# Batch 1 in loaded token order, tails of two batches transposed together, and a new order of the work around them

## The chip, the core and the metric

The kernel runs on one core of a Trainium2 chip. TensorE (PE) multiplies matrices into PSUM, which has eight banks of 128 x 512 float32 per core here; VectorE (DVE), ScalarE (ACT) and GpSimd (POOL) work on tiles in SBUF, the first two also on PSUM. SyncE (SP) and other engines' queues issue transfers (DMA). Each engine runs its own instructions in the order in which they were written, and waits for others by semaphores. The metric is the device time of one execution in microseconds, the median of several; the profile shows one execution, instruction by instruction.

## The reference, cut to what matters

Block-causal attention over 8 batches of 8 heads with 576 tokens of 64 elements, then a gated feed-forward layer over all 4608 tokens.

```python
B, H, S, D = 8, 8, 576, 64
scores = matmul(q, k.T) / sqrt(D)             # per batch and head
scores = where(i // 64 >= j // 64, scores, -1e9)
attn   = exp(scores - max) / (sum + 1e-9)
x      = matmul(attn, v)                      # then (B, S, H*D) -> 4608 x 512
gate   = maximum(x @ w_gate, 0)               # 512 x 1536
val    = x @ w_val                            # 512 x 1536
out    = (gate * val) @ w_out                 # 1536 x 512, float32
```

The order of the tokens matters only where blocks are compared (queries against keys) and in the output rows.

## The kernel before

**Units of work.** A batch has 576 tokens: four full chunks of 128 (the "mains") and 64 more (the "tails"). A head pair is two heads side by side on 128 partitions; there are 32, numbered r = 4 * batch + pair. For each, `scores_all` (before line 480; `scores_of` for batch 0) makes transposed scores with 64-row matmuls (line 464) into three pairs of PSUM banks, ScalarE turns them into exponentials (line 470) in `attnT`, corners above the diagonal are set to zero (`corners`, lines 531 and 532), `head_av` multiplies them with V (line 596; a column of ones gives the sums), and `heads_to_xnat` normalises into `xnat` (lines 544, 545). `to_xT_pe` (line 641) transposes `xnat` on TensorE into `xT`, the feed-forward input with d_model on partitions; from r = 13 on a DMA does it. The tails of batches 0 and 1 have functions of their own: `pe_tails` (line 381) transposes their Q and K, `scores_last` and `scores_tails` make scores, `tails_av` (line 563) and `tails_to_xT` (line 579) the rest. Tails of all batches are gathered in `xTt` and go through the feed-forward layer as a ninth block of 512 tokens.

**The feed-forward layer** is a generator, `ffn_gen` (line 671). For each block of 512 tokens it makes twelve tiles f: four products with `w_gate` and four with `w_val` (line 687) into a pair of banks, relu on ScalarE (line 696), the product of both on VectorE (line 701). Then four output tiles of twelve products each with `w_out` (line 716), copied by VectorE (line 728) and stored. It yields after every four products, so that attention of later batches can be put between: `ffn(n)` runs on to the end of a tile, `ffn_parts(n)` runs n pieces of four. Everything is written out by hand between lines 777 and 977: within an engine, this order is the order of execution.

**Banks.** Banks 0 to 5 are dealt out by `take`, least recently taken first; banks 6 and 7 (`AV`) hold attention outputs and some transposes.

**Loads.** Inputs are float32. They land in a ring of ten `stage` tiles, and POOL casts most of them to bf16 (lines 259, 452, 289, 180). Q, K and V of batches 0 to 3 are loaded with four consecutive tokens per partition (1 KB pieces). A transpose then gives the tokens in the order (j, n), and the copy out of PSUM puts them back in order by reading n and j crosswise (`pe_mains`, line 361). V of batch 1, loaded in the same way, is sorted by products with a selection matrix `sel` (`sort_v`, line 308). The weights come in the order `w_0` (columns 0 to 511 in two halves), `w_1` (columns 512 to 1023, by rows), `w_2`, `w_out`.

**The stretch that the change touches.** After batch 0's attention (up to about 20 us) TensorE runs batch 0's feed-forward work, and between its pieces batch 1's attention (r = 4 to 7), both batches' tails, and the loads and casts of batch 2; from line 926 on a loop over r = 8 to 31 follows, which alternates attention and feed-forward pieces in a fixed pattern.

Of the kernel before, what the change touches and what calls it, by code (L numbers as in the profile page):

```python
# [17 lines left out]
def kernel(  # L18
# [30 lines left out]
    AV = 6  # L49
    taken = [0] * 6  # L50

    def take(n):

        lo = min(range(0, 6, n), key=lambda i: (max(taken[i : i + n]), i))
        taken[lo : lo + n] = [max(taken) + 1] * n
        return banks[:, lo : lo + n, :]

# [42 lines left out]
    sel = consts.tile([128, 2, 516], BF, name="sel")  # L100
# [4 lines left out]
    def constants_tail(i, eng):  # L105

        eng.memset(k_bt[i], 0.0)
        eng.memset(attnT[i][:, :, TAIL + 256 : AW], 0.0)
        eng.memset(attnD[i][:, 256:320], 0.0)
        eng.memset(v_bf[i][:, 4, :, :], 0.0)  # L110
        for hh in range(2):
            eng.memset(v_bf[i][64 * hh : 64 * hh + 64, 4, hh::2, 64:65], 1.0)

    def selection(zero, copy):

        zero(sel, 0.0)
        for c in range(4):
            ps = slice(32 * c, 32 * c + 32)
            copy(
                sel[ps, c % 2].rearrange("p (j m) -> p j m", j=4)[:, :, 0:128:4],  # L120
                ident[ps, None, 32 * c : 32 * c + 32].to_broadcast([32, 4, 32]),
            )

# [34 lines left out]
    class Tails:  # L158


        def load(self):
            self.q, both = new_stage(1024)[0:64], new_stage(1024)
            self.kv = both[:, 0:512], both[:, 512:1024]
            nc.sync.dma_start(
                self.q.rearrange("p (h d) -> p h d", h=16),
                q[0:2, :, 512:576, :].rearrange("b h p d -> p (b h) d"),
            )
            for st, src in zip(self.kv, (k, v)):
                for hh in range(2):
                    nc.sync.dma_start(  # L170
                        st[64 * hh : 64 * hh + 64].rearrange("p (h d) -> p h d", h=8),
                        src[0:2, hh::2, 512:576, :].rearrange("b h p d -> p (b h) d"),
                    )

        def cast(self, b, eng):
            es[b].tl = new_qt()
            eng(es[b].tl, self.q[:, 512 * b : 512 * b + 512])
            for st, diag in zip(self.kv, (k_diag, v_diag)):
                for hh in range(2):
                    eng(  # L180
                        diag(b, hh),
                        st[64 * hh : 64 * hh + 64, 256 * b : 256 * b + 256].rearrange(
                            "p (h d) -> p h d", h=4
                        ),
                    )

    class Early:

        def __init__(self, b):
            self.b = b
            self.m = new_bf()
            self.st = {}
            self.perm = {}
# [67 lines left out]

        def cast_tails(self, engs):
# [21 lines left out]
        def cast_v_packed(self, h0, eng):  # L288
            eng(
                v_p[:, :, 64 * h0 : 64 * h0 + 256].rearrange(  # L290
# [9 lines left out]
        def sort_v(self, h0, engs, out=None):  # L300
# [3 lines left out]
            for odd in range(2):  # L304
                for j in range(4):
                    for g in range(2):
# [4 lines left out]
                            v_p[ps, j, 64 * h0 : 64 * h0 + 256],  # L311
# [39 lines left out]
        def pe_mains(self, hp, evac, out=None):  # L351
            out = out or pair()
            for t in range(2):
# [3 lines left out]
                for j in range(4):  # L357
# [3 lines left out]
                evac[t](  # L361
                    (qTm, kTm)[t][self.b % 2][:, :, hp, :].rearrange(
                        "p c (n j) -> p c n j", j=4
                    ),
                    tp.rearrange("p (j c n) -> p c n j", j=4, c=4),
                )

        def pe_tails(self, evac):

            out = pair()  # L370
            for t in range(2):
                n = (64, 128)[t]
                tp = as_bf(out[:, t, :])[:, 0 : 4 * n].rearrange(
                    "p (h n) -> p h n", h=4
                )
                for hp in range(4):
                    if t == 0:
                        src = self.tl[:, 128 * hp : 128 * hp + 128]
                    else:
                        src = k_bt[self.b % 2][:, hp, :]  # L380
                    nc.tensor.transpose(tp[:, hp, :], src, ident[:n, :n])
                evac[t]((qTt, kTt)[t][self.b % 2], tp)
# [48 lines left out]
    def load_w_half(i, g):  # L431

        sts = []
        for dst, src in ((wg, moe_w_gate), (wv, moe_w_val)):
# [7 lines left out]

    def load_w_in(i):
        cols = slice(512 * i, 512 * i + 512)
        return load_w(wg[i], moe_w_gate[:, cols], 0) + load_w(wv[i], moe_w_val[:, cols], 0)
# [34 lines left out]
    def scores_all(r, tails=True):  # L480
# [3 lines left out]
        sc = [  # L484
            scores(b, hp, pair(), [(0, 0, True)]),
            scores(b, hp, pair(), [(0, 1, True), (384, 3, True)]),
            scores(
                b, hp, pair(),
                [(0, 2, True)]
                + [(256 + 64 * c, c, False) for c in range(4 if tails else 0)],  # L490
            ),
        ]
        for hh in range(2):
            exp(at[:, hh, 0:512], sc[0][:, hh, :])
        exp(at[:, :, 512:1024], sc[1])
        w = 512 if tails else 256
        exp(at[:, :, 1024 : 1024 + w], sc[2][:, :, 0:w])
# [14 lines left out]
    def scores_tails(b):  # L512

        for i in range(2):
# [57 lines left out]
    def tails_of(x):  # L572
# [3 lines left out]
    def tails_to_xT(b, x, evac):  # L576
        tp = as_bf(take(1)[:, 0, :])[:, 0:256].rearrange("p (h n) -> p h n", h=4)
        for hp in range(4):
            nc.tensor.transpose(tp[:, hp, :], x[:, hp, :], ident[:64, :64])
        evac(xTt[:, :, b, :], tp)  # L580
# [35 lines left out]
    def heads_to_xnat(r):  # L616

        blocks = NCH if r >= 8 else 4
        av = banks[:, AV : AV + 2, 0 : 65 * blocks].rearrange(
# [16 lines left out]
    def to_xT_pe(r, evac, bank=None):  # L636
# [3 lines left out]
        for c in range(4):  # L640
            nc.tensor.transpose(br[:, 128 * c : 128 * c + 128], xnat[:, c, :], ident)  # L641
        if b > 1:
            nc.tensor.transpose(br[:, 512:576], xnat[0:64, 4, :], ident[0:64, 0:64])
# [14 lines left out]
    store = []  # L658

    def put(j, s, ob, n0, n1):  # L660
        if j < B:
            r0 = S * j + 128 * s
            (nc.gpsimd if j == 0 else nc.scalar).dma_start(out[r0 : r0 + 128, :], ob)
        else:
            for i in range(2):
# [3 lines left out]
                )  # L669

    def ffn_gen():

        for j in range(B + 1):
# [4 lines left out]
            for fs in groups:  # L678
                out = {f: pair() for f in fs}
                gate = {}  # L680
                steps = [(f, t, c) for f in fs for t in range(2) for c in range(4)]
                if len(fs) > 1:

                    steps.sort(key=lambda step: (step[2] == 3, step[1], step[2]))
# [14 lines left out]
                for f in fs:  # L699
                    h = sb.tile([128, 512], BF, name="hT", bufs=15)  # L700
# [3 lines left out]
                    hT.append(h)  # L704
                yield True
            todo = [[o] for o in outs(j)]
            if j == 0:

                todo = [outs(0)[0:2]] + todo[2:]
            for group in todo:  # L710
                ops = take(len(group))
# [14 lines left out]
                for g, (s, n0, n1) in enumerate(group):  # L726
                    ob = sb.tile([128, 512], FP, name="ob", bufs=3)[:, 0 : n1 - n0]
# [3 lines left out]
                    store.append(lambda j=j, s=s, ob=ob, n=(n0, n1): put(j, s, ob, *n))  # L731
                yield True
# [22 lines left out]
    def ffn_parts(n):  # L755

        for _ in range(n):
            assert next(gen) is False
# [16 lines left out]
    with tc.manual_schedule(engines={E.PE, E.DVE, E.Activation, E.Pool, E.SP}):  # L775
# [7 lines left out]
        w_0 = [load_w_half(0, g) for g in range(2)]  # L783
        w_1 = load_w_in(1)
# [4 lines left out]
        e0.cast_qk(0, 2, (dve, act))  # L789
        e0.pe_mains(0, (dve, act), banks[:, 4:6])  # L790
        junk(2, banks[:, 7])
        constants(1, nc.gpsimd)
        constants_tail(1, nc.gpsimd)
        for h0 in (2, 4, 6):
# [211 lines left out]
```

## Time and profile before

| | us |
|---|---|
| median of 3 runs (369.71 to 371.03) | 369.93 |
| the profiled execution | 370.19 |
| its span, first to last instruction | 368.4 |
| TensorE busy in it | 355.9 |
| VectorE, ScalarE, POOL busy | 165.6, 170.6, 116.2 |

The granted TensorE clock is 1.00 throughout.

How to read the lines that follow. A row of the order of time begins with its start and its length in us, then engine and source line, operation, output and inputs, shape, and how many instructions it joins; in brackets stands how long the engine was idle before, and what ended that. PE is the matmuls, PEld the weight loads that run beside them. A row of a group ends with total busy time and mean ns of one. A row by stretch has the stretch, its length, the busy time of PE, PEld, DVE, ACT and POOL (with counts), the granted clock, the busy share of the DMA engines, and GB/s.

### The profile page before, as it was taken

The page shows a single profiled execution, that of the slowest core. Times are in us where ns is not written, and L with a number is a line of the kernel's source. Part 1 is how long each engine was busy: PE and PEld are TensorE (multiplying, and loading weights), DVE is VectorE, ACT ScalarE, POOL GpSimd, SP SyncE. Part 2 cuts the span into 40 slices and gives each one's busy share as a digit, 9 for nine tenths or more (in the row PEclk, how much of TensorE's full clock was granted, in tenths as well). Part 3 has the DMA queues.
Part 4 walks back from the last instruction along what each step waited for, and adds up shares of the span by engine and source line. Part 5 has one row for each costly group of instructions (what it writes and reads, how often), then busy time and mean ns, then how long its engine had stood idle before and what let it go on. Part 6 is the DMA issues. An engine that isn't in the chain of part 4 may idle for free.

```text
span 368.4 us, 7471 instructions
## 1 busy us (share of the span) xinstructions
PE 355.9 (97%) x2954; PEld 187.1 (51%) x2993; DVE 165.6 (45%) x329; ACT 170.6 (46%) x268; POOL 116.2 (32%) x161
## 2 busy tenths in 40 slices
PE   6889999999999999999999999999999999999995
PEld 2634455556555555555555555555555544444443
DVE  5744444376475543444334443444344433423422
ACT  5833738656665653455445543644364403302310
POOL 5767768175898205810391022000000000000000
PEclk9999999999999999999999999999999999999999
DMA  8999999979999979997599829073201130020013
GB/s 255 289 371 354 376 203 332 165 198 231 195 186 140 140 136 77 179 97 147 87 179 91 137 78 136 19 143 70 88 16 18 46 101 1 3 85 28 2 38 104
DMA packets 139891, 51.02 MB, mean 138 GB/s; under 512 B 119504, under 2 KB 133072, under 8 KB 139856
## 3 DMA queue, kind: packets, MB, share of 16 engines
q1 hardware_dynamic: 78448, 34.29, 40.7%
q0 software_dynamic: 56704, 8.13, 39.9%
q10 hardware_dynamic: 4704, 8.13, 6.3%
q8 instruction: 23, 0.38, 0.5%
q14 instruction: 12, 0.10, 0.1%
HBM read 37.75 MB, written 9.44 MB: 128 GB/s over the span
## 4 chain that ended last, share of the span: by engine, by line
PE 89%; DMA 5%; SPq 2%; ACT 1%; issue 1%; POOL 1%; DVE 0%; ACTq 0%; DVEq 0%; POOLq 0%
PE banks L687 48%; PE banks L716 25%; PE banks L596 7%; PE banks L464 6%; DMA stage<-in_moe_w_val_dram 3%; SPq L223 1%; DMA stage<-in_v_dram 1%; DMA stage<-in_k_dram 1%; PE banks L563 1%; PE banks L308 1%; PE banks L358 1%; ACT attnT L470 0%; PE banks L641 0%; DVE ob L728 0%; POOL wv L452 0%
## 5 line engine op out<-in xcount | busy, mean ns | idle before, releaser
L470 ACT ACTIVATE attnT<-banks 128x1024 bf16<-128x1024 f32 (+1 forms) x118 | 84.9, 804 | 61.8 <-PE banks L464 56.2
L696 ACT ACTIVATE gate_sb<-banks 128x512 bf16<-128x512 f32 x108 | 64.9, 603 | 104.9 <-PE banks L687 104.2
L701 DVE TENSOR_TENSOR hT<-gate_sb,banks 128x512 bf16<-128x512 bf16 x108 | 74.1, 688 | 81.9 <-PE banks L687 77.6
L687 PE MATMUL banks<-xT,wv 128*128 128x512 bf16 x379 | 98.6, 379 | 1.6 <-POOL wv L452 1.2
L687 PE MATMUL banks<-xT,wg 128*128 128x512 bf16 x363 | 97.4, 379 | 1.8 <-ACT v_p L470 0.4
L716 PE MATMUL banks<-wo,hT 128*128 128x512 bf16 (+1 forms) x433 | 96.3, 373 | 0.6
L687 PEld LDWEIGHTS <-wv 128*128 128x128 bf16 x432 | 42.0, 98 | 52.8 <-POOL wv L452 2.8
L716 PEld LDWEIGHTS <-hT 128*128 128x128 bf16 x444 | 42.3, 98 | 46.1
L687 PEld LDWEIGHTS <-wg 128*128 128x128 bf16 x432 | 40.4, 98 | 45.8 <-issue 1.0
L728 DVE COPY ob<-banks 128x512 f32<-128x512 f32 (+1 forms) x37 | 25.1, 677 | 56.2 <-PE banks L716 56.1
L406 POOL DMA_DIRECT2D v_bf<-in_v_dram x16 | 14.3, 904 | 67.5 <-PE banks L596 67.5
L596 PEld LDWEIGHTS <-attnT 128*128 128x128 bf16 x792 | 29.2, 98 | 9.1 <-issue 1.3
L596 PE MATMUL banks<-v_bf,attnT 128*128 128x65 bf16 x792 | 33.6, 194 | 0.2 <-DVE qTm L361 0.2
L464 PE MATMUL banks<-qTm,kTm 64*128 64x512 bf16 (+3 forms) x256 | 25.3, 299 | 2.1 <-ACT attnT L470 1.2
L545 DVE TENSOR_TENSOR xnat<-banks,recip 128x640 bf16<-128x640 f32 (+2 forms) x36 | 25.9, 721 | 1.2
L464 PEld LDWEIGHTS <-kTm 64*128 64x128 bf16 x512 | 16.9, 94 | 11.2 <-issue 1.7
L544 DVE RECIPROCAL recip<-banks 128x10 f32<-128x10 f32 (+3 forms) x38 | 8.0, 210 | 31.4 <-PE banks L596 29.7
L531 DVE MEMSET attnT<- 64x192 uint32 x28 | 6.1, 218 | 19.5 <-ACT attnT L470 18.9
L406 POOL DMA_DIRECT2D k_bf<-in_k_dram x16 | 14.2, 929 | 1.2 <-DMA v_bf<-in_v_dram 1.2
L406 POOL DMA_DIRECT2D q_bf<-in_q_dram x16 | 14.4, 927 | 0.4 <-DMA v_bf<-in_v_dram 0.4
L687 PE MATMUL banks<-xTt,wg 128*128 128x512 bf16 x48 | 12.3, 379 | 0.1
L687 PE MATMUL banks<-xTt,wv 128*128 128x512 bf16 x46 | 12.0, 379 | 0.1
(98 smaller groups left out, 203.2 us busy)
## 6 DMA issues: line engine op xcount, KB each, us to landing
out_dram<-ob ACTq DMA_DIRECT2D x28, 256.0 KB, 2.2
stage<-in_moe_w_gate_dram SPq DMA_DIRECT2D x6, 512.0 KB, 9.4
stage<-in_moe_w_val_dram SPq DMA_DIRECT2D x6, 512.0 KB, 9.7
stage<-in_q_dram SPq DMA_DIRECT2D x6, 512.0 KB, 7.1
stage<-in_k_dram SPq DMA_DIRECT2D x6, 512.0 KB, 8.5
stage<-in_moe_w_out_dram SPq DMA_DIRECT2D x6, 512.0 KB, 9.1
stage<-in_v_dram SPq DMA_DIRECT2D x8, 256.0 KB, 6.0
q_bf<-in_q_dram POOLq DMA_DIRECT2D x16, 128.0 KB, 6.6
```

The source lines that it names most:

```text
L406: nc.gpsimd.dma_start(dst, src[b, :, 128 * c : 128 * c + n, :].rearrange("h p d -> p h d"),)
L464: nc.tensor.matmul(o, kTm[b % 2][ps, c, hp, :], x, start=True, stop=True)
L470: nc.scalar.activation(out, sc, AF.Exp, scale=scale)
L531: eng.memset(three[:, :, :, 0:64], 0.0)
L544: nc.vector.reciprocal(recip, av[:, :, :, 64])
L545: nc.vector.tensor_tensor(out=out, in0=av[:, :, :, 0:64], in1=recip.to_broadcast([rows, heads, n, 64]), op=AX.mult,)
L596: nc.tensor.matmul(av[:, 0, p, :], w, vb[:, c, h, :], start=(p == 0), stop=(c == p), skip_group_check=True,)
L687: nc.tensor.matmul(out[f][:, t, :], (wg, wv)[t][i][:, c, fo : fo + 128], x[:, c, :], start=(c == 0), stop=(c == 3),)
L696: nc.scalar.activation(gate[f], out[f][:, 0, :], AF.Relu)
L701: nc.vector.tensor_tensor(out=h, in0=gate[f], in1=out[f][:, 1, :], op=AX.mult)
L716: nc.tensor.matmul(ops[:, g, 0 : n1 - n0], hT[f][:, 128 * s : 128 * (s + 1)], wo[i][:, f % 4, n0:n1], start=(f == 0), stop=(f == 11),)
L728: nc.vector.tensor_copy(ob, ops[:, g, 0 : n1 - n0])
```

## The change

Line numbers below are those of the profile of before, unless said.

1. **Loaded order for batch 1.** Q and K of batch 1 are copied out of PSUM in an order in which each half chunk of 64 tokens keeps the order (j, n) of its load (`AS_LOADED`); `sel` sorts V into the same order. Blocks of 64 tokens are what the mask compares, so nothing else changes until `to_xT_pe`, which for batch 1 multiplies with a permuted identity `order` and so puts tokens back. POOL builds `order` with one copy at the start.
2. **Tails of batches 0 and 1.** Their Q and K are loaded with four tokens per partition in 1 KB pieces, cast into one `perm` tile, and transposed by eight 128 x 128 transposes (`Tails.pe`) in place of sixteen; six copies on VectorE take them out of PSUM. `kTt` is therefore zeroed at the start (one more memset on DVE, one on POOL). The normalised tails of both batches share one tile `xt` and four transposes.
3. **Whole transposes.** For batches 2 and 3 the fifth transpose of `to_xT_pe` takes all 128 rows.
4. **Weights.** `w_1` is loaded and cast in column halves, as `w_0` and `w_2` are.
5. **Start.** The first K cast is split between ScalarE and POOL, and the copy of the first K in two; one weight cast moves ahead of a V cast on POOL.
6. **The order between batch 0's attention and the loop** is rewritten: batch 1's attention moves earlier and between other feed-forward pieces, `ffn(n)` is replaced by `parts(n)`, eight more products are done ahead of the loop, several copies move from ScalarE to VectorE. `take` skips banks that the feed-forward generator holds. For batch 1 the first two tiles run the products with input rows 0 to 255 first.
7. **Stores and buffers.** The stores of block 0 go from POOL's queue to ScalarE's; `ob` has 4 buffers (3), `hT` 13 (15).

The diff, cut to its core:

```diff
+    AS_LOADED = {(1, hp) for hp in range(4)}
+    def token_order(copy):
+        copy(order.rearrange("p (h n j) -> p h j n", h=2, j=4),
+             ident.rearrange("p (h j n) -> p h j n", h=2, j=4))
...
+        def pe(self, evac):
+            out = pair()
+            for t in range(2):
+                tp = as_bf(out[:, t, :])[:, 0:512]
+                for j in range(4):
+                    nc.tensor.transpose(
+                        tp[:, 128 * j : 128 * j + 128], self.bf[:, t, j, :], ident)
+                tp = tp.rearrange("p (j n b h) -> p j n b h", j=4, b=2, h=4)
+                for b in range(2):
+                    for hh in range(2) if t else (0,):
+                        ps = slice(64 * hh, 64 * hh + 64) if t else slice(0, 128)
+                        dst = kTt[b][ps, :, ps] if t else qTt[b]
+                        evac[t](dst.rearrange("p h (n j) -> p h n j", j=4),
+                                tp[ps, :, :, b, :].rearrange("p j n h -> p h n j"))
...
+                    if (self.b, hp) in AS_LOADED:
+                        dst = dst.rearrange("p c (h j n) -> p c h j n", h=2, j=4)
+                        src = tp.rearrange("p (j c h n) -> p c h j n", j=4, c=4, h=2)
...
-            nc.tensor.transpose(br[:, 512:576], xnat[0:64, 4, :], ident[0:64, 0:64])
+            nc.tensor.transpose(br[:, 512:640], xnat[:, 4, :], ident)
...
-        w_1 = load_w_in(1)
+        w_1 = [load_w_half(1, g) for g in range(2)]
...
-        e0.cast_qk(0, 2, (dve, act))
-        e0.pe_mains(0, (dve, act), banks[:, 4:6])
+        e0.cast_first((dve, act, pool))
+        e0.pe_mains(0, (dve, act), banks[:, 4:6], first=True)
...
+        parts(3)
+        cast_w(w_out[0], pool)
+        e1.pe_mains(0, (dve, dve), banks[:, AV : AV + 2])
+        cast_w(w_out[1], pool)
+        parts(1)
+        e1.load_qk(4, 4)
+        e1.pe_mains(1, (act, dve), banks[:, AV : AV + 2])
+        cast_w(w_out[2], pool)
+        scores_all(4, False)
+        parts(3)
+        corners(4, nc.vector)
+        parts(1)
+        e1.cast_qk(4, 4, (pool, pool))
+        e1.sort_v(0, (act, dve), banks[:, AV : AV + 2])
+        scores_all(5, False)
+        heads_av(4)
+        parts(1)
+        e1.load_v_packed(4)
+        corners(5, nc.vector)
+        parts(1)
+        heads_av(5)
+        parts(1)
+        tails.load()
+        tails.cast_qk(pool)
+        to_xT_pe(4, (act,), None)
+        parts(3)
+        e1.cast_v_packed(4, pool)
+        parts(2)
...
+        e1.pe_mains(2, (dve, dve), banks[:, AV : AV + 2])
+        parts(1)
+        e1.pe_mains(3, (dve, dve), banks[:, AV : AV + 2])
+        scores_all(6, False)
+        tails.pe((dve, dve))
+        corners(6, nc.vector)
+        to_xT_pe(5, (act,), banks[:, AV + 1])
+        scores_all(7, False)
+        e1.sort_v(4, (dve, dve), banks[:, AV : AV + 2])
+        parts(1)
+        corners(7, nc.gpsimd)
+        tails.cast_v(1, pool)
+        parts(2)
+        heads_av(6)
+        scores_last(0)
+        scores_tails(0, (0,))
+        scores_tails(0, (1,))
...
+        to_xT_pe(6, (act,), None)
+        e2.cast_tails((pool, pool))
+        heads_av(7)
+        parts(1)
```

More of the change, by code (lines that the diff above doesn't have):

```diff
@@ L50, with hold @@
     taken = [0] * 6
+    held = set()
     def take(n):
-        lo = min(range(0, 6, n), key=lambda i: (max(taken[i : i + n]), i))
+        free = [i for i in range(0, 6, n) if not held & set(range(i, i + n))]
+        lo = min(free, key=lambda i: (max(taken[i : i + n]), i))
         taken[lo : lo + n] = [max(taken) + 1] * n
+        last[:] = range(lo, lo + n)
         return banks[:, lo : lo + n, :]
+    last = []
+    def hold(bank):
+        held.update(last)
+        return bank
     def pair():
@@ L194, in __init__ @@
             self.b = b
+            self.v_p = (wo[2], v_p)[b % 2]
             self.m = new_bf()
@@ L349, in unpermute, with pe_mains @@
                 )
-        def pe_mains(self, hp, evac, out=None):
+        def pe_mains(self, hp, evac, out=None, which=(0, 1), first=False):
             out = out or pair()
-            for t in range(2):
+            for t in which:
                 tp = as_bf(out[:, t, :])[:, 0:512]
```

310 lines of the change are left out of this document (157 added, 153 removed).

## The prediction, made before the changed kernel ran

> **What bounds the kernel now.** I read the page's busy times and its chain of waits first, then busy times by stretch, then TensorE's order of time from 20 to 90 us, because that is where the diff sits.
>
> ```profile
> PE 355.9 (97%) x2954; PEld 187.1 (51%) x2993; DVE 165.6 (45%) x329; ACT 170.6 (46%) x268; POOL 116.2 (32%) x161
> ...
> PE 89%; DMA 5%; SPq 2%; ACT 1%; issue 1%; POOL 1%; DVE 0%; ACTq 0%; DVEq 0%; POOLq 0%
> ...
> 28.00:86.00 58.00, 56.40 (x574) 31.40 (x583) 28.08 (x57) 32.02 (x54) 36.11 (x45) 1.00 1.01 271
> 86.00:151.00 65.00, 64.57 (x626) 35.59 (x629) 33.76 (x66) 35.90 (x59) 37.62 (x49) 1.00 1.66 154
> ```
>
> TensorE is the bound: 97% busy and 89% of the chain, at a granted clock of 1.00 in both stretches. So an edit can gain in two ways only: fewer or cheaper TensorE instructions, or less waiting of TensorE. After 86 us almost nothing waits (64.57 busy of 65.00), so nothing done there by other engines is worth time. Between 28 and 86 us the busy share hides some waiting, because a matmul's busy time runs past the start of the next one; I therefore read gaps from start to start.
>
> **Part 1: the weights of columns 512 to 1023 (`w_1`) come in column halves.** Before, four transfers bring row halves, so the first feed-forward tile of these columns (f=4) needs all four.
>
> ```profile
> 25.21 1.03 PE L687 MATMUL banks<-xT,wg 128*128 128x512 bf16 x4
> 26.68 0.60 PE L687 MATMUL banks<-xT,wv 128*128 128x512 bf16 x2 [0.44 <-POOL wv L452]
> 28.04 0.60 PE L687 MATMUL banks<-xT,wv 128*128 128x512 bf16 x2 [0.76 <-POOL wv L452]
> 28.48 1.03 PE L687 MATMUL banks<-xT,wg 128*128 128x512 bf16 x4
> 29.34 1.03 PE L687 MATMUL banks<-xT,wv 128*128 128x512 bf16 x4
> ...
> 22.61 0.54 PEld L687 LDWEIGHTS <-wv 128*128 128x128 bf16 x4 [0.61 <-POOL wv L452]
> 22.86 1.04 POOL L452 CAST wg<-stage 128x1024 bf16<-128x1024 f32 x1 [0.31 <-DMA stage<-in_moe_w_gate_dram]
> 26.94 1.04 POOL L452 CAST wv<-stage 128x1024 bf16<-128x1024 f32 x1 [0.32 <-DMA stage<-in_moe_w_val_dram]
> 32.96 1.04 POOL L259 CAST k_bf<-stage 128x1024 bf16<-128x1024 f32 x1 [0.46 <-DMA stage<-in_k_dram]
> ...
> 20.00:24.00 4.00, 3.83 (x18) 1.62 (x18) 1.96 (x4) 1.68 (x3) 3.13 (x3) 1.00 1.05 385
> 28.00:32.00 4.00, 3.96 (x19) 1.84 (x20) 1.38 (x2) 1.20 (x2) 2.63 (x3) 1.00 1.10 348
> ```
>
> Four products take 0.864 us (28.48 to 29.34), so eight take 1.73. The eight of f=4 run from 25.21 to 28.48, 3.27 us: 1.54 us are waits for casts, and the casts wait for loads. After, f=4 and f=5 need only the first two transfers. They land about where the first two land now (the first cast starts at 22.86); the second is cast by about 25.6, and its first use is at 25.21 + 0.86 = 26.07. The gain is the whole 1.54 us.
>
> Its cost: rows of a half are 1 KB long where they were 2 KB. The stretch with 2 KB pieces moves 385 GB/s and the one with 1 KB pieces 348, which is 1.36 against 1.51 us per 512 KB. Four transfers make every later load some 0.6 us late. The nearest user is the first K transpose of batch 1: 44 products after 25.21, plus four transposes, at 34.94. Its cast ends at 34.00 now and would end at 34.6, so 0.3 us of cover are left.
>
> **The opening** I cost at nothing. VectorE gets a memset and a wider one ahead of the first Q cast (0.3 us later), the first K cast and its copy are split (about 0.3 us sooner). Whatever comes of it ends at f=2, whose weight loads wait until 22.61 for a cast that only the loads set. TensorE's idle before that row is the cover; an opening later by more would cost its excess one for one.
>
> **Part 2: fewer and whole transposes on TensorE.** Tails of batches 0 and 1: sixteen transposes, half of them 64 rows high, become eight whole ones. The two last groups of four become one. In batch 2 the fifth transpose of a head pair becomes 128 rows high.
>
> ```profile
> 35.39 0.39 PE L358 MATMUL banks<-ident,q_bf 128*128 128x128 bf16 x4
> 35.61 0.39 PE L358 MATMUL banks<-ident,k_bf 128*128 128x128 bf16 x4
> ...
> 61.59 0.29 PE L381 MATMUL banks<-ident,q_bt 64*128 64x64 bf16 x4
> 61.81 0.40 PE L381 MATMUL banks<-ident,k_bt 128*128 128x128 bf16 x4
> ...
> 62.80 0.38 PE L641 MATMUL banks<-ident,xnat 128*128 128x128 bf16 x4
> ...
> 88.49 0.39 PE L641 MATMUL banks<-ident,xnat 128*128 128x128 bf16 x4
> ...
> 88.94 1.04 PE L687 MATMUL banks<-xT,wg 128*128 128x512 bf16 x4
> ```
>
> Four whole transposes issue in 0.22 us (35.39 to 35.61). The sixteen take 61.59 to 62.80, 1.21 us; eight whole ones take 0.45: gain 0.76. Four narrow ones take the same 0.22 (61.59 to 61.81), so one group less is 0.22. A group of four whole and one narrow takes 0.45 (88.49 to 88.94); five whole take 0.28: 0.17 each, four times 0.68. Together 1.66 us. TensorE is the bound, so all of it counts. The permuted identity replaces the plain one in the same count of instructions: nothing.
>
> **Part 3: the order of batch 1.** The work is the same; what counts is where TensorE waits. Waits that go away, from starts:
>
> ```profile
> 44.26 0.88 PE L464 MATMUL banks<-qTm,kTm 64*128 64x512 bf16 x8
> 45.07 0.48 PE L596 MATMUL banks<-v_bf,attnT 128*128 128x65 bf16 x10
> ...
> 59.84 1.11 PE L464 MATMUL banks<-qTm,kTm 64*128 64x512 bf16 x8
> 60.88 0.78 PE L596 MATMUL banks<-v_bf,attnT 128*128 128x65 bf16 x20
> ...
> 63.51 0.65 PE L464 MATMUL banks<-qTt,kTm 64*128 64x64 bf16 x32
> 64.09 0.78 PE L596 MATMUL banks<-v_bf,attnT 128*128 128x65 bf16 x20
> 64.71 0.38 PE L687 MATMUL banks<-xT,wg 128*128 128x512 bf16 x1
> 65.46 1.24 PE L687 MATMUL banks<-xT,wg 128*128 128x512 bf16 x4 [0.37 <-ACT v_p L470]
> ...
> 70.72 0.86 PE L464 MATMUL banks<-qTt,kTm 64*128 64x64 bf16 x32
> 71.73 0.81 PE L687 MATMUL banks<-xT,wg 128*128 128x512 bf16 x3 [0.16 <-issue]
> ```
>
> Eight score products take 0.81 us unhindered (44.26 to 45.07) and 1.04 at 59.84: 0.23 lost. One product from 64.71 to 65.46 takes 0.75 where 0.216 is due: 0.54. Thirty-two small ones take 0.58 at 63.51 and 1.01 at 70.72: 0.43. Sum 1.20 us, all where tails and two head pairs are crowded behind ScalarE.
>
> Waits that come, because score blocks now follow each other with less between them. The prices hang on these rows:
>
> ```profile
> 60.26 2.49 ACT L470 ACTIVATE attnT<-banks 128x512 bf16<-128x512 f32 x4 [1.32 <-PE banks L464]
> ...
> 62.62 0.48 DVE L382 COPY qTt<-banks 128x256 bf16<-128x256 bf16 x2
> ...
> L361 DVE COPY qTm<-banks 128x512 bf16<-128x512 bf16 x7 | 4.8, 689 | 3.6 <-PE banks L358 3.5
> ...
> L644 DVE COPY xT<-banks 128x512 bf16<-128x512 bf16 x3 | 1.3, 425 | 3.1 <-PE banks L641 3.0
> ```
>
> The exponentials of a head pair start 0.42 us after its scores (59.84, 60.26) and last 2.49. Bounded from both sides, by laying these durations behind the changed order: f=10 takes the banks of the first scores of head pair 4 (0.2 to 0.5); the heads of pair 4 follow the V sort at once (0 to 0.3); those of pair 5 need its last exponential and the zeroing of its corners (0.1 to 0.45); the new tail transposes take the banks of the first scores of pair 6 (0.3 to 0.7); the scores of pair 7 take those of its other scores and of the tails' six copies (0.5 to 1.25); transposing pair 6 right behind its heads needs the normalised tile (0.2 to 0.6); the first product of batch 2 now follows the last transpose of its input directly (0.1 to 0.35). Ends: 1.4 and 4.15 us. The like waits above measure 0.23, 0.54 and 0.43, about 0.4 each; these stand at five places (score blocks of pairs 4 and 5, tails, pair 7, batch 2), so I take 2.0.
>
> One assumption in it: Q and K copies of batch 1 are now read in runs of 16 elements, and I let them take the 425 ns of the contiguous xT copy, not the 689 ns of the old one.
>
> A rule that speaks against this part: the Trainium skill, page TensorEngine Tiling (Array Packing), section PSUM Bottleneck, says to empty PSUM with both ScalarE and VectorE. The change gives both copies of three of batch 1's four head pairs and all six tail copies to VectorE. By my rows that costs no more than the 2.0; by the rule it goes to the upper end, 4.15, which is the second rival below.
>
> POOL loses four stores (ScalarE issues them; between the head pairs it has nothing to do), and the tails' Q and K come in 1 KB pieces instead of 256 B; both only move loads that have slack now.
>
> **Sum.** 1.54 + 1.66 + 1.20 - 2.0 = 2.4 us gained. The profiled execution took 370.19 us with a span of 368.4; it would take 367.8. The median of the runs is 369.93, so I predict 367.5.
>
> **Rivals.** First, *the waits are covered* (chance 0.22): ScalarE and VectorE are about half busy, and between the blocks stand feed-forward products. Only 0.6 us of new waits remain: gain 3.8, 366.1 us. Against it: the score blocks of pairs 6 and 7 have no feed-forward product between them. Second, *the change doesn't quicken the copies, and VectorE and PSUM banks bind* (0.14): copies stay at 689 ns, every new wait goes to its upper end. Gain 4.40 - 4.15 = 0.25: 369.7. Third, *slower: the tails' load takes over* (0.22).
>
> ```profile
> 49.06 1.04 POOL L259 CAST k_bf<-stage 128x1024 bf16<-128x1024 f32 x1 [0.94 <-DMA stage<-in_k_dram]
> ...
> 53.39 0.87 POOL L180 CAST k_bt<-stage 64x256 bf16<-64x256 f32 x2
> ...
> 56.28 0.41 POOL L180 CAST v_bf<-stage 64x256 bf16<-64x256 f32 x1 [1.56 <-DMA stage<-in_v_dram]
> ```
>
> Batch 1 now runs earlier, close behind its loads. POOL casts the tails' Q and K ahead of the second V half, and TensorE transposes them at about 54.4 (from 25.21, 27.6 us of issue and 1.6 of waits lie ahead of them). Casting two tiles of 512 takes some 1.25 us, so it decides from a landing later than 53.2. The last tail piece lands at 56.2 now; had the new ones landed there, 0.6 late, they would be ready at 58.1: 3.7 us lost, net 1.3 slower, 371.2; each further 0.6 us adds as much. For it: K of the second half is cast only at 49.06, 0.94 us after POOL was free. Against it: the larger pieces, and the tails' K was being cast at 53.39 already.
>
> **Chances.** My forecast has 0.42, with its own range 366.2 to 368.9. Half a percent (1.85 us) is about what a measurement of this kernel can tell from no change: below 368.1 is faster, above 371.8 slower. Faster: 0.22 + three quarters of 0.42 = 0.54. Slower: 0.15 of the third rival (landing later still) and 0.02 of the second: 0.17. Same: 0.29. The range runs from 365.3 (all waits covered and the opening helping) to 371.3 (the tails' load): about 2 in 10 lie outside.
>
> **What would show it.** Part 1: f=4's two groups of value products start back to back, with no wait for POOL at 26 to 28 us. Part 2: eight transposes of the tails within 0.45 us, no 64-row forms among transposes. Part 3: gaps before f=10, the tail transposes, the scores of pair 7; Q and K copies of batch 1 near 425 ns. It is wrong if TensorE waits over 1 us for POOL between 45 and 60 us, if the opening no longer meets the 22.61, or if gaps appear after 86 us.

## The result and the profile after

The changed kernel takes 374.43 us (median of 11 runs, 372.80 to 376.76), the kernel before 370.23 in the same rounds (369.62 to 373.71): a ratio of 1.0104, 95% interval 1.0071 to 1.0137. It is slower by 4.2 us where I had forecast 2.4 us faster. The profiled execution took 375.84 us with a span of 374.1, against 370.19 and 368.4.

The page of the changed kernel, first the busy times, then the granted clock and the DMA engines in 40 slices, then the chain of waits:

```profile
PE 358.4 (96%) x2981; PEld 188.1 (50%) x2981; DVE 166.7 (45%) x335; ACT 166.9 (45%) x263; POOL 114.0 (30%) x158
...
PEclk9999999999999999899999999999999999999999
DMA  8999999989999969997299749245301130020013
...
PE 78%; DMA 14%; DVE 3%; SPq 2%; issue 1%; ACT 1%; POOL 1%; ACTq 0%; DVEq 0%; POOLq 0%
```

TensorE's part of the chain fell from 89% to 78% and that of DMA rose from 5% to 14%. One slice of the clock, the seventeenth (150 to 159 us), is below full. Busy times by stretch, the granted clock third from the end:

```profile
28.00:86.00 58.00, 54.68 (x565) 30.93 (x565) 30.08 (x62) 29.51 (x48) 31.98 (x40) 1.00 1.03 268
86.00:151.00 65.00, 63.32 (x600) 34.21 (x597) 32.17 (x66) 35.02 (x57) 37.60 (x47) 1.00 1.62 157
151.00:160.00 9.00, 8.16 (x69) 4.42 (x69) 2.71 (x6) 4.60 (x7) 6.51 (x9) 0.81 2.40 159
```

TensorE's waits put together (us in total, how often, the longest):

```profile
PE banks L752 <- DMA xT<-xnat: 3.8, 3, 2.1
PE banks L232 <- ACT attnT L520: 1.1, 1, 1.1
```

Line 752 is the feed-forward product, and it waits three times, 3.8 us in all, for a DMA transpose of its input: after 86 us, where I had ruled waits out. TensorE's order of time, after and then before, at the first of the three:

```profile
143.43 0.28 PE L551 MATMUL banks<-qTt,kTt 128*128 128x64 bf16 x4
143.75 5.34 PE L782 MATMUL banks<-wo,hT 128*128 128x512 bf16 x24
148.93 0.81 PE L752 MATMUL banks<-xT,wg 128*128 128x512 bf16 x3
151.84 0.38 PE L752 MATMUL banks<-xT,wg 128*128 128x512 bf16 x1 [2.10 <-DMA xT<-xnat]
152.06 1.64 PE L752 MATMUL banks<-xT,wv 128*128 128x512 bf16 x4
```

```profile
144.51 0.28 PE L503 MATMUL banks<-qTt,kTt 128*128 128x64 bf16 x4
144.62 5.34 PE L716 MATMUL banks<-wo,hT 128*128 128x512 bf16 x24
149.81 0.59 PE L596 MATMUL banks<-v_bf,attnT 128*128 128x65 bf16 x14
...
151.59 1.03 PE L687 MATMUL banks<-xT,wg 128*128 128x512 bf16 x4
```

The first rows of both are the same event, the last tail scores of batch 4, with the same number of feed-forward products done (408 of them by the counts, since each call runs on to the end of a tile). There the changed kernel is 1.08 us ahead. Then both make two output tiles (24 products). Before, attention of the next head pair follows, and block 3's first tile starts at 151.59. After, that tile stands right behind the output tiles, at 148.93, and its fourth product needs the last quarter of its input. That comes by a DMA transpose, which is issued later as well. Its issue before, and then after:

```profile
143.24 1.20 SPq L651 DMA_TRANSPOSE xT<-xnat  x1
```

```profile
144.75 1.20 SPq L707 DMA_TRANSPOSE xT<-xnat  x1
```

The attention whose result is transposed stood ahead of an output tile before (12 products from 141.92) and stands behind one now. The DMA view of 143 to 146 us of the changed kernel gives the time from issue to landing last:

```profile
xT<-xnat SPq DMA_TRANSPOSE x1, 7.0
```

The need came 2.66 us sooner (152.24 before, 149.58 after) and the landing 1.74 us later (150.06, 151.80; 1.51 of that is the later issue). Before, 2.18 us were to spare. So TensorE stops 2.26 us, counted from start to start. Then products that are due every 0.216 us come more slowly (four from 152.06 to 153.49, 1.43 us where 0.86 is due).

The distance between these tail scores, batch by batch, shows the whole loss:

| from the tail scores of batch | 4 to 5 | 5 to 6 | 6 to 7 | 7 to TensorE's end |
|---|---|---|---|---|
| before, us | 38.36 | 38.37 | 38.36 | 105.03 |
| after, us | 42.41 | 39.86 | 39.32 | 105.24 |
| lost, us | 4.05 | 1.49 | 0.96 | 0.21 |

Lost are 6.71 us; less the 1.08 that it was ahead, 5.63, which with rounding is the difference of the spans (5.7). The first batch pays most: 2.26 for the stop, 0.2 between lines 551 and 782 (each batch pays this), and 1.6 for work at the lower clock.

### The profile page after: what moved, and what is told of

Its sections match the earlier page's. It is cut to its first block, busy times and chain, and to the rows that moved or that the text cites. A ratio compares the mean times of both kernels' runs of the same rounds, so it can differ in the third digit from the quotient of the medians.

```text
span 374.1 us, 7485 instructions
## 1 busy us (share of the span) xinstructions
PE 358.4 (96%) x2981; PEld 188.1 (50%) x2981; DVE 166.7 (45%) x335; ACT 166.9 (45%) x263; POOL 114.0 (30%) x158
## 4 chain that ended last, share of the span: by engine, by line
PE 78%; DMA 14%; DVE 3%; SPq 2%; issue 1%; ACT 1%; POOL 1%; ACTq 0%; DVEq 0%; POOLq 0%
PE banks L752 45%; PE banks L782 18%; PE banks L648 7%; PE banks L514 5%; DMA stage<-in_moe_w_val_dram 5%; DMA xT<-xnat 5%; DMA kTt<-k_bt 2%; SPq L279 2%; DMA stage<-in_moe_w_gate_dram 1%; DVE xnat L593 1%; DMA stage<-in_k_dram 1%; ACT attnT L520 1%; PE banks L611 1%; PE banks L373 0%; DVE ob L794 0%
## 5 line engine op out<-in xcount | busy, mean ns | idle before, releaser
L752 PE MATMUL banks<-xT,wg 128*128 128x512 bf16 x384 | 100.1, 379 | 4.8 <-DMA xT<-xnat 3.8
L752 PE MATMUL banks<-xT,wv 128*128 128x512 bf16 x384 | 100.0, 381 | 0.0
```

What stands on the lines that cost most here:

```text
L752: nc.tensor.matmul(out[f][:, t, :], (wg, wv)[t][i][:, c, fo : fo + 128], x[:, c, :], start=(c == 0), stop=(c == 3),)
```

## The experiments

**The eight products.** The change does 192 feed-forward products ahead of the loop, before did 184; a block has 144, and the loop's pattern places tiles by count. So the eight decide on which side of a head pair's attention an output tile, and then block 3's first tile, falls. Two experiments move only them. In the changed kernel the lead is given back:

```diff
+        done[0] -= 8
         for r in range(8, 4 * B):
```

> The changed kernel with its count of feed-forward products set back by 8 ahead of the loop, so that from the loop's first head pair on every feed-forward tile stands where it stood before the change. Nothing else differs. Theory (the eight products' lead moves the first tile of blocks 3, 4 and 5 onto a transposed input that is still in flight, and the 2.3 us stop lowers the clock): the stops of 2.26, 1.28 and 0.74 us at lines 752 behind xT and the 1.75 us of the lower clock go, span 374.1 - 6.0 = 368.1, ratio to before 0.992 to 0.998. Rival (the loss is made by the waits between 52 and 64 us and by ScalarE's stores): within 1 us of 374.1, ratio near 1.010.

In the kernel before it is added:

```diff
+        ffn(8)
         for r in range(8, 4 * B):
```

> The kernel before with 8 feed-forward products more ahead of the loop and nothing else, so that its tiles in the loop stand where the change puts them. Theory: the same stops appear, some 2, 1.3 and 0.7 us at blocks 3, 4 and 5, with a lower clock behind the first, and the ratio is 1.010 to 1.017 (370.2 + 4 to 6). Rival: the loop does not care where the tiles stand, ratio 0.998 to 1.002.

The lead added to the kernel before makes it slow: 375.29 us, ratio 1.0141 (1.0085 to 1.0197), with stops of 1.54, 1.20 and 0.84 us at the same places. The first of them, in the order of time:

```profile
152.02 0.38 PE L687 MATMUL banks<-xT,wg 128*128 128x512 bf16 x1 [1.37 <-DMA xT<-xnat]
```

The stretch behind it:

```profile
152.00:156.00 4.00, 3.93 (x56) 2.50 (x57) 1.55 (x3) 2.47 (x4) 3.11 (x5) 1.00 2.13 180
```

So the eight products alone make a loss of the size seen, with no other part of the change. The transpose is issued 2.42 us later than before (145.66) and needed 1.76 sooner (150.48). The clock did not fall behind this stop of 1.54 us, though I had expected it to.

The lead given back took away all three stops and 4 us, but not as much as expected: 370.48 us, ratio 0.9981 (0.9944 to 1.0017). The profiled execution is the slowest of its ten (372.43; the fastest took 368.80), so not each of them need look like it. Its order of time has a new stop, early, and the stretch behind that a lower clock:

```profile
102.80 0.72 PE L514 MATMUL banks<-qTm,kTm 64*128 64x512 bf16 x8
105.71 0.29 PE L514 MATMUL banks<-qTt,kTm 64*128 64x64 bf16 x8 [2.19 <-DMA qTt<-q_bt]
```

```profile
105.00:109.00 4.00, 3.07 (x28) 1.61 (x29) 2.14 (x5) 1.31 (x2) 2.06 (x4) 0.66 2.60 144
```

Batch 3's transposed query tails (qTt) landed at 105.67. The kernel before needs them at 104.99 and has them at 104.21: 0.78 us to spare. Here they are needed at 103.35, and they also landed 1.46 us later than before (issued 0.79 later, 0.67 longer on the way). So a kernel that is over 0.8 us faster up to here waits, unless they come sooner too. In the changed kernel the eight products put that need off to 105.76, and the tails are there at 105.40: good at 104 us, bad at 149.

**The lead for that stretch only.** If so, it should be kept until 130 us and then given back.

```diff
             corners(r, nc.vector)
+            if r == 14:
+                done[0] -= 8
             ffn(12 if r < 13 else 8)
```

> The changed kernel; the eight products stay ahead through the end of batch 3's loads and are given back at head pair 14, so that from 130 us on the tiles stand as before. Theory (the lead is useful at 104 us, where the tail transposes of batch 3 land late, and harmful from 149 us on): no stop over 0.5 us at 104 us, none at 149, 191 and 231, clock 1.00, span 368.4 - 1.1 = 367.3, ratio 0.995 to 0.998. Rival (the lead only moves the stops, other stops come in their place): ratio 1.000 or more.

It took 368.64 us, ratio 0.9956 (0.9933 to 0.9979): 0.4% faster than before, clear of the interval, and no gap over 0.3 us on TensorE from 90 us on, at a clock of 1.00. The transpose issued at 141.66 still took 5.9 us; nothing waits for it, since block 3 starts at 150.01, behind attention:

```profile
148.22 0.59 PE L648 MATMUL banks<-v_bf,attnT 128*128 128x65 bf16 x14
...
150.01 1.03 PE L752 MATMUL banks<-xT,wg 128*128 128x512 bf16 x4
```

**Why the transpose takes 7 us.** At the same time GpSimd's queue loads the next V, Q and K. The first try moved the load of V one head pair later in the program.

```diff
-                if hp == 0:
+                if hp == 1:
                     load_qkv(b + 1, (2,))
```

> The changed kernel with the loads of the next V (GpSimd's queue) issued one head pair later, so that they no longer run beside the transposes of xT at the end of a block. Theory A (the transpose of xT is slow because these loads share the DMA engines): it lands in about 3 us instead of 7, the three stops and the lower clock go, ratio 0.990 to 0.998 although the eight products stay ahead. Theory B (the transpose is slow for itself, or from the queue it is in): the stops stay above 1.5 us at block 3, ratio 1.007 to 1.013.

The stop stayed (2.36 us; 373.82 us, ratio 1.0089, 1.0058 to 1.0120), but this told nothing of the transpose, for the loads did not move. GpSimd's order of time, first of the changed kernel, then of this one:

```profile
143.77 3.52 POOL L459 DMA_DIRECT2D v_bf<-in_v_dram  x4 [19.24 <-PE banks L551]
```

```profile
142.68 3.53 POOL L459 DMA_DIRECT2D v_bf<-in_v_dram  x4 [20.41 <-PE banks L551]
```

GpSimd stands 19 us at this load, until TensorE has passed the heads that read the old V. The buffer sets the time, not the place in the program. The second try therefore gave the load something to wait for: a copy of two columns that reads the transposed input.

```diff
                 if hp == 0:
+                    pool(seen, xT_of(b - 1)[:, 3, 0:2])
                     load_qkv(b + 1, (2,))
```

> The changed kernel; a copy of two columns on GpSimd that reads the last transposed input of a block stands ahead of the loads of the next V from head pair 16 on, every fourth pair. So those loads, and the Q and K loads behind them in the same queue, start only when that transpose has landed. The eight products stay ahead. Theory (the transpose takes 7 us because these loads share the DMA engines with it): it lands within 3.5 us of its issue, before 148.5, the stops at blocks 3, 4 and 5 fall under 0.3 us each, clock 1.00, span 368.5, ratio 0.995 to 1.000. Rival (the transpose is slow by itself): it lands 6 to 7 us after its issue as now, ratio 1.008 to 1.013.

The next kernel has this and, ahead of the Q and K loads of batch 4, a like copy that reads the last tail transpose of batch 3:

```diff
+            if r == 11:
+                pool(seen, kTt[1][:, 0, 0:2])
             if hp == 3 and b + 2 < B:
```

> As the kernel with the loads held, and besides the Q and K loads of batch 4 start only when the last tail transpose of batch 3 has landed. Theory (the transposes at 97 to 106 us are slow from the same sharing): the tail transposes of batch 3 land within 3.5 us of their issue instead of 6 to 8, no stop at 109; 0.2 to 0.6 us better than with the later loads alone, ratio 0.994 to 0.999. Rival: no difference, or the held loads of batch 4 come late for their own transposes at head pair 14 and cost over 1 us near 130 us.

With the lead left as the change has it, 369.94 us, ratio 0.9998 (0.9982 to 1.0015), and with both loads held 369.32, ratio 0.9991 (0.9975 to 1.0007). The three stops are gone, but the gain does not come through whole: in the profiled execution with the later loads held the tail scores of batch 4 stand 1.33 us ahead of before (143.18), and each batch behind them takes 0.2 us more (38.57, before 38.36). From the DMA views, the time from issue to landing with the later loads held (xT) and with both held (qTt, kTt), then the same tail transposes of the changed kernel:

```profile
xT<-xnat SPq DMA_TRANSPOSE x1, 3.9
```

```profile
qTt<-q_bt SPq DMA_TRANSPOSE x1, 2.3
kTt<-k_bt SPq DMA_TRANSPOSE x1, 2.8
```

```profile
qTt<-q_bt SPq DMA_TRANSPOSE x1, 6.0
kTt<-k_bt SPq DMA_TRANSPOSE x1, 8.2
```

Beside the loads these transposes take about two to three times as long. The held loads then run beside later transposes instead (one issued at 162.21 takes 5.6 us, the same one 2.4 in the changed kernel), for which nothing waits. That holding the second group of loads gained anything in the whole time is not shown: the two intervals overlap.

**The clock.** Ten products that nobody reads were put into the wait, in a bank that the tile clears afterwards.

```diff
                 for n, (f, t, c) in enumerate(steps):
+                    if (j, f, t, c) == (3, 0, 0, 3):
+                        junk(10, out[f][:, 1, :])
```

> The changed kernel with ten products that nobody reads (an identity against zeros, 512 columns, into the bank that the tile clears afterwards) ahead of the product that waits 2.26 us for xT of block 3. They compute nothing of the output. They only keep TensorE at work during the wait. Theory (the stop lowers the granted clock, which costs another 1.75 us): the wait's time stays, as 2.2 us of work, the clock stays 1.00 in the 8 us behind it, span 374.1 - 1.75 = 372.3, ratio 1.003 to 1.008. Rival (the clock fell by itself, or from something else at 152 us): the clock falls again, ratio 1.009 to 1.013.

By the whole time this can't be told from the changed kernel (373.69 us, ratio 1.0097, 1.0068 to 1.0125). The trace tells it: the stretch from 152 to 156 us of the changed kernel, then of this one, and this one's order of time.

```profile
152.00:156.00 4.00, 4.00 (x42) 2.34 (x41) 0.69 (x1) 1.45 (x3) 2.71 (x4) 0.57 2.13 174
```

```profile
152.00:156.00 4.00, 3.95 (x57) 2.53 (x57) 1.73 (x3) 2.92 (x5) 3.03 (x5) 1.00 2.18 170
```

```profile
149.19 2.32 PE L833 MATMUL banks<-zeros,ident 128*128 128x512 bf16 x10
151.57 0.38 PE L754 MATMUL banks<-xT,wg 128*128 128x512 bf16 x1
```

The granted clock is 1.00 in place of 0.57, and from the tail scores of batch 4 to those of batch 5 it takes 40.95 us in place of 42.41. With the wait still there as work, 1.46 us are the clock's in these two executions.

The drop does not stand in every execution. Of the changed kernel's eleven, seven have a mean granted clock of 0.991 to 0.995 (median 375.15 us) and four 0.998 to 1.000 (373.60), so most of the loss stays without it. With the wait filled one of eight has 0.993 and seven 0.998 or more; of 35 executions of the kernel before, three have 0.995. That filling the wait keeps the clock up is therefore likely, but not shown by the one profile.

**Does a gain ahead of 100 us reach the end?** First the column halves of `w_1` alone, in the kernel before:

```diff
-        w_1 = load_w_in(1)
+        w_1 = [load_w_half(1, g) for g in range(2)]
...
-        cast_w(w_1, pool)
+        for w in w_1:
+            cast_w(w, pool)
```

> The kernel before with the weights of columns 512 to 1023 in column halves and nothing else. Up to 30 us the theory and its rival agree: f=4's waits go and TensorE is 1.5 us ahead. Theory (the tail transposes of batch 3, which land at 104.21 and are used at 104.99, are set by the loads and do not come sooner): only 0.8 us of the 1.5 is left at the end, and a stop of some 0.7 us stands at the small score products near 103 us; span 367.6, ratio 0.997 to 0.999. Rival (TensorE alone sets the end, as in my prediction): the whole 1.54 us, span 366.9, ratio 0.994 to 0.997.

Then the same with the Q and K loads of batch 4 held:

```diff
+            if r == 11:
+                pool(seen, kTt[1][:, 0, 0:2])
             if hp == 3 and b + 2 < B:
```

> The kernel before with the column halves and with the Q and K loads of batch 4 held in the same way. Theory: with the cap at 104 us removed the whole 1.5 us of the halves reaches the end, span 366.9, ratio 0.994 to 0.997, and no stop near 103. Rival (the stop with the halves alone came from somewhere else): a stop of over 1 us near 103, ratio 0.997 or more.

Then the changed kernel with the lead given back and those loads held:

```diff
+        done[0] -= 8
         for r in range(8, 4 * B):
...
+            if r == 11:
+                pool(seen, kTt[1][:, 0, 0:2])
             if hp == 3 and b + 2 < B:
```

> The changed kernel with the eight products given back ahead of the loop (tiles as before from the first loop pair on) and the Q and K loads of batch 4 held until the tail transposes of batch 3 have landed. Theory (the given-back lead failed alone only because those transposes land at 105.7): they land near 100, no stop near 103, and the whole gain made ahead of 100 us reaches the end: span 366.0 to 366.9, ratio 0.991 to 0.996. Rival (something else holds head pair 12): a stop of 1 us or more near 103 remains, ratio 0.997 or more.

The halves alone: 369.89 us, ratio 0.9982 (0.9947 to 1.0017), where the theory put it, though the interval takes in most of the rival's range too. In its profiled execution (374.11, the second slowest of ten; eight lie between 368.6 and 370.5) the cap took more than the gain, a stop of 3.9 us (order of time) with the clock at 0.57 behind it (by stretch):

```profile
107.52 0.40 PE L464 MATMUL banks<-qTt,kTm 64*128 64x64 bf16 x8 [3.71 <-DMA qTt<-q_bt]
```

```profile
107.00:111.00 4.00, 3.48 (x30) 2.00 (x30) 2.07 (x4) 1.02 (x1) 1.83 (x3) 0.57 2.80 102
```

Halves and held loads: 369.50, ratio 0.9966 (0.9942 to 0.9991). No stop is left near 103, and the ratio lies in the theory's range, yet 0.6 us of the 1.5 arrive, not all. The profiled execution, the slowest of its twelve (370.32), shows two places where the gain goes: the first K transposes of batch 1, which wait for a cast (0.58 us more than usual from start to start; my prediction had left 0.3 us of cover there), and the same stop as at 103, one batch earlier (0.90 us in the same way).

```profile
34.87 0.40 PE L358 MATMUL banks<-ident,k_bf 128*128 128x128 bf16 x4 [0.42 <-POOL k_bf L259]
...
78.45 0.29 PE L464 MATMUL banks<-qTt,kTm 64*128 64x64 bf16 x8 [0.73 <-DMA qTt<-q_bt]
```

So neither theory held here. The third kernel has the lowest median: **368.12 us, ratio 0.9940 (0.9918 to 0.9962)**, 2.0 us under before. That it beats the one whose lead is given back at 130 us (0.9956) is not shown, since their intervals overlap. The tail transposes land 2.6 and 2.8 us after their issue, and nothing waits:

```profile
101.42 0.39 PE L693 MATMUL banks<-ident,xnat 128*128 128x128 bf16 x4
101.65 0.22 PE L699 MATMUL banks<-ident,xnat 128*128 128x128 bf16 x1
101.70 0.58 PE L648 MATMUL banks<-v_bf,attnT 128*128 128x65 bf16 x14
...
102.25 0.72 PE L514 MATMUL banks<-qTm,kTm 64*128 64x512 bf16 x8
102.80 0.28 PE L514 MATMUL banks<-qTt,kTm 64*128 64x64 bf16 x8
```

**The waits between 52 and 60 us.** In the changed kernel the tail transposes wait 1.1 us for the exponentials of head pair 6. All engines there:

```profile
53.49 1.13 ACTq L720 DMA_DIRECT2D out_dram<-ob  x2
53.57 0.72 PE L514 MATMUL banks<-qTm,kTm 64*128 64x512 bf16 x8
...
54.59 0.61 POOL L213 CAST perm<-stage 128x512 bf16<-128x512 f32 x1 [0.43 <-DMA stage<-in_k_dram]
54.73 1.08 ACT L520 ACTIVATE attnT<-banks 128x512 bf16<-128x512 f32 x2 [6.54 <-DVE kTm L435]
...
55.37 0.87 PE L232 MATMUL banks<-ident,perm 128*128 128x128 bf16 x8 [1.09 <-ACT attnT L520]
56.08 0.39 PE L693 MATMUL banks<-order,xnat 128*128 128x128 bf16 x4
56.78 0.97 PE L514 MATMUL banks<-qTm,kTm 64*128 64x512 bf16 x7 [0.31 <-ACT attnT L520]
58.33 0.27 PE L514 MATMUL banks<-qTm,kTm 64*128 64x256 bf16 x1 [0.57 <-DVE kTt L240]
```

Two stores stand ahead of the exponentials on ScalarE, and the tails' K is cast late. One kernel puts the stores back on GpSimd:

```diff
-    STORE = nc.scalar
+    STORE = nc.gpsimd
```

> The changed kernel with block 0's stores back in GpSimd's queue; the phase stays as the change has it, so only the stretch 52 to 60 us is compared. Theory A (ScalarE's exponentials of head pair 6 start 0.7 us late because two store instructions stand ahead of them, and that alone holds the tail transposes): exponentials start at 54.0 in place of 54.7, tail transposes at 54.6 in place of 55.4, gain 0.7 us there. Theory B (the tails' late K cast holds the K half of these transposes nearly as long): the exponentials start sooner but the last tail transpose ends within 0.3 us of where it does now.

Another does this on top of the kernel of 368.12 us, splits the tails' load and moves its Q and K part ahead of V:

```diff
+        tails.load_qk()
         e1.load_v_packed(4)
...
-        tails.load()
+        tails.load_v()
```

> As the kernel with the lead given back and the loads held, and besides block 0's stores go out by GpSimd and the tails' Q and K are loaded ahead of the second half of V. Theory (the tail transposes at 54 to 56 us wait for ScalarE's late exponentials and for the tails' late cast together): with both moved the 1.1 to 1.3 us wait ahead of them falls to 0.3 to 0.6, 0.5 to 0.9 us better than with the lead given back and the loads held alone, ratio 0.989 to 0.994. Rival: the wait moves on to the exponentials of pairs 6 and 7 and nothing is gained, ratio as there.

With the stores on GpSimd the exponentials start 0.48 us behind their scores (53.94, 54.42), not 1.16 (53.57, 54.73), and the tail transposes' idle time falls from 1.09 to 0.41 us: theory A. But in the kernel of 368.12 us, where the stores stand on ScalarE and are issued at 52.69, it is 0.41 as well. The second kernel has the same 0.41 and the same two waits behind it, and takes 368.46 us, ratio 0.9949 (0.9924 to 0.9974): nothing gained, as its rival said. So the stores cost 0.7 us in the one execution of each that was profiled and nothing in another, and the late load nothing.

## Why the prediction was wrong

**The step that failed** is the sentence "After 86 us almost nothing waits (64.57 busy of 65.00), so nothing done there by other engines is worth time", with its companion in the third part, which costed the move of the feed-forward work by its first product alone (0.1 to 0.35 us). No wait in a profile means that a transfer arrives in time, not that it has time to spare. Before, the input's last quarter landed at 150.06 and was needed at 152.24, 2.18 us later, and the tail queries had 0.78 us. I listed eight more products ahead of the loop and did not follow them to where they move the work: an output tile ahead of the attention whose result is transposed, so that the transpose starts 1.51 us later, and block 3's first tile ahead of the next head pair, so that the input is needed 2.66 us sooner. The order of the two programs would have shown both. My list of what would prove me wrong did name gaps after 86 us.

**Missing, too, was the clock.** In the profiled execution a stop of 2.26 us cost 3.85, because of the work behind it.

**Part 1 was right.** After, f=4 and f=5 run back to back, with no wait:

```profile
25.16 1.03 PE L752 MATMUL banks<-xT,wg 128*128 128x512 bf16 x4
26.03 1.03 PE L752 MATMUL banks<-xT,wv 128*128 128x512 bf16 x4
26.89 1.03 PE L752 MATMUL banks<-xT,wg 128*128 128x512 bf16 x4
27.75 1.03 PE L752 MATMUL banks<-xT,wv 128*128 128x512 bf16 x4
```

f=5 starts at 26.89 where it started at 28.48, 1.59 us sooner (1.54 predicted), and the opening cost nothing, since f=4 starts at 25.16 and 25.21.

**Part 2 was right** where nothing stands in its way: five whole transposes issue in 0.28 us (101.42 to 101.70 above). In the changed kernel they do so at three of the four places, all in batch 2; at the fourth, 88.82, they take 0.48. The tails' eight were held up by ScalarE and took 0.71 (55.37 to 56.08).

**Part 3 had both sides too small.** On VectorE the Q and K copies of batch 1 take 412 to 424 ns in place of 680 to 691, as I assumed, so the rival that hangs on slow copies had the wrong cause. The six tail copies are slow, though: 406 to 428 ns for 256 elements per partition, for which a contiguous copy took 280 before.

But the added waits that I can read off are larger than my 2.0, and than the 4.15 of the upper end. From start to start, less the usual issue time, they are 0.57 (f=10, behind a weight cast and not behind banks), 0.31, 0.45, 1.27 and 0.27 (tails), 0.47, 0.38 and 0.75 (pair 7), 0.40 (pair 6): about 4.9. Of them 0.75 stand behind the six tail copies that VectorE makes alone. The rule that I weighed there, to empty PSUM with both ScalarE and VectorE, is that of the Trainium skill, page TensorEngine Tiling (Array Packing), section PSUM Bottleneck. The trace bears on it with this 0.75 alone, and no run shares those copies. Some 2.4 stand behind exponentials.

The removed waits were more than 1.20 as well: my "0.81 unhindered" for eight score products was itself hindered, for they issue in 0.55 (102.25 to 102.80 above). The net is what counts. At the loop's start (77.46 after, 77.03 before, with eight products or 1.73 us more done) the change is 1.30 us ahead. Part 1 (1.59) and what Part 2 gains up to there (0.76 and 0.22) make 2.57, so Part 3 cost about 1.27 net, where I had 0.6 up to there.

**The sum** was thus not far off: 2.4 predicted, and in the kernel that keeps the change and takes away the two collisions, 2.0 measured (368.12). In part that is luck: both sides of Part 3 were too small and nearly made up for each other, and that kernel also makes loads wait, which the prediction did not have. The rival in which the tails' load takes over had a true premise: its K landed at 54.46, later than 53.2. But it did not decide, as loading it sooner showed.

## What to carry to other kernels

Before moving work, list the transfers that arrive only just before the later work needs them, with the slack of each (need less landing), and follow a moved count through every loop that places work by counting. A gain on the bounding engine reaches the end only as far as the transfers behind it come sooner too; here the wait for transposed tail queries capped it twice, at 78 and at 104 us. Here a transfer that was needed soon became two to three times faster when bulk loads were made to wait for it, by a dummy read, while moving their issue in the program did nothing, because a buffer held them.

## What the runs showed of the hardware

A stop of TensorE of 2.2 to 2.4 us was followed by some 3 us at about half the clock (0.57 to 0.72 granted over 4 us) in each of four profiled executions, and one of 3.9 us in a fifth; a stop of 1.54 us was not (1.00). By the mean clock the changed kernel has the drop in seven of eleven executions. The Trainium skill, page TensorE: Matmul & The Clock Gate, section Why this matters for your kernels, advises against idle gaps of over about 3 us. Here the clock fell behind a stop of 2.26 us, 2.10 of them idle.

The DMA transpose of block 3's last input quarter (128 x 512 in bf16) landed 3.3 and 3.9 us after its issue in the two kernels that hold GpSimd's loads there, and 5.9 to 7.2 us beside the loads. The median of the changed kernel's twenty such transposes is 2.9.

A copy out of PSUM with its source read in runs of 16 elements took 412 to 424 ns on VectorE, as long as a contiguous one (425); read crosswise, element by element, 680 to 692.
